# An attention and MoE kernel on one core: another order of issue in its first chunk

## The chip, the core and the metric

The kernel runs on one core of a Trainium2 chip. Its engines take their instructions each in its own order: TensorE (PE) multiplies, ScalarE (ACT), VectorE (DVE) and GpSimd (POOL) do elementwise work, and SyncE (SP) issues the DMAs. The metric is the device time of one execution in microseconds. Before the change the runs gave 989.86, 989.25 and 988.27 us, a median of 989.25.

## The reference

For each of 8 batches and 8 heads, attention over 576 tokens of 64 values, where a token sees only few others: in heads 0 to 3 the 32 tokens up to itself, in heads 4 to 7 every fourth of the last 128. The result is the input x of a mixing layer of low rank and of a two-layer perceptron:

```python
scores = scale * np.matmul(q, k.transpose(0, 1, 3, 2))
scores = np.where(masks[None], scores, -1e9)          # windows of 32, plain or dilated by 4
attn = softmax(scores)
x = np.matmul(attn, v)                                # to (8, 576, 512)
h = x.transpose(0, 2, 1) @ U @ V                      # U: 576 x 32, V: 32 x 576
u = x + h.transpose(0, 2, 1)
out = u + np.maximum(u @ w_ch1, 0.0) @ w_ch2          # 512 -> 2048 -> 512
```

U, V and the two weights come as 64-bit floats, the rest as 32-bit floats.

## The kernel before

**The perceptron** sets the frame. The 36 tiles of 128 tokens are worked in 12 chunks: chunk 0 holds 4 tiles, chunk 1 two, the others three. The 2048 hidden values are 16 blocks, f = 0 to 15. For each chunk and f, `layer1` makes `ph` (one PSUM tile) in three groups of four matmuls, w1h by uth, w1l by uth, w1h by utl: weights and data are each split in a rounded high part and the rest, so that three products stand for one exact one. ACT makes `hh` (the rounded relu of ph), DVE makes `hl` (the rest). `layer2` of the block before then adds into the accumulators `acc`, three matmuls per tile of tokens. So an f is 12 matmuls of ph and 12 of acc in chunk 0.

**The weights** are made in chunk 0 while they are first used. A piece (`raw`, 64-bit words, w1 or w2 of one f, in turn) is fetched by SP, four raw buffers in all. ACT narrows both halves of its words (L199, L203), DVE shifts (L207), DVE (for w1) or POOL (for w2) adds (L209), then the high part is cast (w1h on ACT, L213; w2h on DVE, L215) and POOL takes the low part as the difference (L216). `weight_step` runs twice per f; it finishes one piece, adds the next, and narrows the one after. The 64-bit U and V take the same way: the last of them is a piece called uv, number 2, whose parts `fetch_rest`, `narrowed(2)`, `add_low(2)` and `finish(2)` are put in by hand.

**Attention.** Batch 0 is worked ahead of chunk 0. Batch 1 is worked in chunk 0, in nine blocks of 64 rows twice by four heads: scores `s` (L416), on DVE the masked row maxima `nmax` (L435), on ACT the exponentials `p` (L439), on PE the turned `ptp` (L450), a copy to `pt` (DVE, L456), the product with v, `pv` (L473), and on DVE a division by the row sums (L479 to L503). Rows of the dilated heads are scattered to their tokens by DMAs from `xp` into x (L516, SP).

**The mixing layer.** For each batch and each half c of the columns: `split_x` makes xhl, a high part on ACT (L529) and a low one on POOL or DVE (L531), for five tiles of tokens; `t_mm` multiplies them with U into one PSUM tile t (L561); `t_evict` turns t into ts with three ACT casts and one DVE subtraction in turn (L570 to L577); `mix` multiplies ts with V into m (L585), and DVE adds it to x (L587). The first half of batch 0's x (dilated heads) leaves as xp to a buffer in DRAM (`leave`, "spare", L813) and comes back in order of tokens (`come`, L818) before mix(0, i, 1) adds to it.

**What sets the order.** A list `queue` holds pairs of a position and a step of work. In chunk 0, `slot()` is called 109 times, between the groups of matmuls of layer1 and between tiles of layer2. It counts a position up from 0, by 4/(3 x 109) = 0.0122 per slot, and each time issues all steps of the queue whose position has been reached. An f is 6.8 slots. What the list issues stands on every engine at that place. Batch 1's part is made by `batch_items`: its attention blocks start at STEP0 and follow at STEP1 = 0.075, and its mixing layer starts, for each half, at AFTER's first number, with AFTER's second number between one step and the next. Work on PSUM goes through one set of three buffers ("ps") for s, ptp, pv, t and m.

## Time and profile before

The profiled execution took 991.13 us, of which the span from its first to its last instruction is 989.30; the granted TensorE clock was 0.968 of full speed in the mean.

| stretch, us from the start | length | PE busy | DVE | ACT | POOL |
| --- | --- | --- | --- | --- | --- |
| 0 to 43.34: batch 0's attention, ph_0 | 43.34 | 37.76 | 25.66 | 28.44 | 20.07 |
| 43.34 to 166.84: the rest of chunk 0 | 123.50 | 115.89 | 92.69 | 68.73 | 78.70 |
| 166.84 to the end: chunks 1 to 11 | 822.46 | 816.13 | 468.39 | 283.72 | 232.99 |

Names in the profile are those of the program without buffer numbers; "[1.30 <-ACT ts L577]" behind an instruction says that its engine was idle for 1.30 us before it, until ACT's instruction of line 577 ended. Where numbers are kept, as below, ph0_1 is chunk 0's ph of f=1, and x_436 one buffer of x. A line such as "x16" stands for that many instructions in a row.

### The profile page before, as it was taken

To read this page: it belongs to the slowest core of one execution; us is meant where nothing else is said; L and a number is where in the kernel's file an instruction comes from. 1 tells how busy PE (TensorE), PEld (TensorE's weight loads), DVE (VectorE), ACT (ScalarE), POOL (GpSimd) and SP (SyncE) were. 2 spreads that over 40 slices of the span, in tenths; PEclk is the share of its full clock that TensorE was granted. 3 is DMA by queue.
4 is the path that set the end of the run, shared out by engine and by line. 5 is a ranking of instruction groups with operands and counts; after the bars stand their busy time and mean duration, and the time that the engine had idled before them with its cause. 6 is when DMAs were issued, how large, how long until landed. Compare 5 with 4: busy or idle time off the path is not lost.

```text
span 989.3 us, 18075 instructions
## 1 busy us (share of the span) xinstructions
PE 969.8 (98%) x5941; PEld 844.2 (85%) x5941; DVE 586.7 (59%) x1969; ACT 380.9 (38%) x936; POOL 331.8 (34%) x555
## 2 busy tenths in 40 slices
PE   9898999999999999999999999999999999999998
PEld 7576778888888888888888888888898888999997
DVE  5676787777377758766377745776557773311211
ACT  6654654454244424343144432435233531111110
POOL 4575656354143514253042521335122620000000
PEclk9899999999999999999999999999999999999999
DMA  9476644344244316343233413443243412200000
GB/s 332 139 243 200 200 158 132 106 138 115 54 129 133 103 45 172 108 129 96 70 99 91 136 57 89 136 125 84 71 102 101 135 56 53 86 1 1 32 1 32
DMA packets 100188, 106.15 MB, mean 107 GB/s; under 512 B 12480, under 2 KB 85376, under 8 KB 100096
## 3 DMA queue, kind: packets, MB, share of 16 engines
q1 hardware_dynamic: 100096, 105.01, 36.1%
q8 instruction: 48, 0.79, 0.3%
q14 instruction: 44, 0.36, 0.1%
HBM read 82.94 MB, written 17.89 MB: 102 GB/s over the span
## 4 chain that ended last, share of the span: by engine, by line
PE 79%; DMA 2%; DVE 2%; SPq 0%; issue 0%; POOL 0%; ACT 0%; DVEq 0%; POOLq 0%; ACTq 0%
PE ph L965 35%; PE acc L982 35%; PE pv L473 3%; PE s L403 3%; PE t L561 2%; DMA zd<-z 1%; PE m L585 1%; PE s L416 1%; DMA qkr<-qk 0%; DVE pt L462 0%; DVE x L1012 0%; DMA x<-xp 0%; SPq L634 0%; DVE v L209 0%; DVE z L630 0%
## 5 line engine op out<-in xcount | busy, mean ns | idle before, releaser
L982 PE MATMUL acc<-w2h,hh 128*128 128x512 f32 x576 | 227.4, 395 | 0.0
L982 PE MATMUL acc<-w2l,hh 128*128 128x512 f32 x576 | 227.3, 395 | 0.0
L380 POOL TENSOR_TENSOR qks<-qkr,qks 128x160 fp32r<-128x160 f32 x192 | 103.8, 541 | 328.4 <-ACT qks L379 242.3
L982 PE MATMUL acc<-w2h,hl 128*128 128x512 f32 x576 | 213.0, 395 | 0.2 <-DVE hl L971 0.2
L971 DVE SCALAR_TENSOR_TENSOR hl<-ph,hh 128x384 fp32r<-128x384 f32 (+2 forms) x192 | 106.3, 554 | 177.4 <-ACT hh L970 176.5
L970 ACT ACTIVATE hh<-ph 128x384 fp32r<-128x384 f32 (+2 forms) x192 | 93.5, 487 | 264.3 <-PE ph L965 255.2
L965 PE MATMUL ph<-uth,w1h 128*128 128x384 f32 (+2 forms) x768 | 170.6, 340 | 4.3 <-ACT w1h L213 3.6
L965 PE MATMUL ph<-utl,w1h 128*128 128x384 f32 (+2 forms) x768 | 172.6, 338 | 0.0
L965 PE MATMUL ph<-uth,w1l 128*128 128x384 f32 (+2 forms) x768 | 170.5, 339 | 0.2 <-POOL w1l L216 0.2
L439 ACT ACTIVATE p<-p,nmax 128x160 f32<-128x160 f32 (+1 forms) x288 | 109.6, 406 | 130.7 <-DVE nmax L435 129.3
L965 PEld LDWEIGHTS ph<-uth,w1h 128*128 128x128 f32 x768 | 135.9, 188 | 22.3 <-ACT w1h L213 4.9
L462 DVE STREAM_TRANSPOSE pt<-p 32x128 f32<-32x128 f32 x432 | 130.1, 301 | 18.6 <-ACT p L439 13.3
L965 PEld LDWEIGHTS ph<-uth,w1l 128*128 128x128 f32 x768 | 133.6, 189 | 4.3 <-POOL w1l L216 1.3
L965 PEld LDWEIGHTS ph<-utl,w1h 128*128 128x128 f32 x768 | 133.4, 188 | 3.8 <-issue 0.2
L982 PEld LDWEIGHTS acc<-w2h,hl 128*128 128x128 f32 x576 | 107.7, 188 | 22.6 <-DVE hl L971 0.6
L982 PEld LDWEIGHTS acc<-w2h,hh 128*128 128x128 f32 x576 | 108.2, 188 | 16.2
L982 PEld LDWEIGHTS acc<-w2l,hh 128*128 128x128 f32 x576 | 108.3, 188 | 15.8 <-issue 0.2
L379 ACT CAST qks<-qkr 128x288 fp32r<-128x288 f32 x192 | 81.0, 429 | 103.7 <-PE s L403 54.5
L383 POOL TENSOR_TENSOR qks<-qkr,qks 64x128 fp32r<-64x128 f32 x192 | 90.5, 471 | 15.0
L432 DVE TENSOR_TENSOR p<-s,wide_sb 128x160 f32<-128x160 f32 x192 | 59.5, 320 | 57.0 <-PE s L403 54.4
L531 POOL TENSOR_TENSOR xhl<-x,xhl 128x256 fp32r<-128x256 f32 (+1 forms) x65 | 47.6, 741 | 83.1 <-ACT xhl L529 73.8
L435 DVE CUSTOM_DVE_ANT_0 p<-s,p 128x160 f32<-128x160 f32 x192 | 59.8, 320 | 3.7
(89 smaller groups left out, 875.8 us busy)
## 6 DMA issues: line engine op xcount, KB each, us to landing
qkr<-qk SPq DMA_DIRECT2D x192, 144.0 KB, 2.2
v<-vv SPq DMA_DIRECT2D x126, 130.0 KB, 2.4
raw<-w SPq DMA_DIRECT2D x26, 512.0 KB, 4.1
out<-x SPq DMA_DIRECT2D x36, 256.0 KB, 2.4
zd<-z SPq DMA_DIRECT2D x120, 64.0 KB, 2.1
xt<-zd SPq DMA_DIRECT2D x30, 256.0 KB, 2.8
k<-qk SPq DMA_DIRECT2D x18, 320.0 KB, 5.6
raw<-w SPq DMA_DIRECT2D x12, 256.0 KB, 3.4
```

Of the source, the lines that this page charges most:

```text
L379: nc.scalar.copy(out=t[:, 0:QK2], in_=raw)
L380: nc.gpsimd.tensor_tensor(out=t[:, QK2:], in0=raw[:, P:], in1=t[:, P:QK2].bitcast(F32), op=ALU.subtract)
L383: eng.tensor_tensor(out=t[lo, 0:P], in0=raw[lo, 0:P], in1=t[lo, 0:P].bitcast(F32), op=ALU.subtract)
L432: nc.vector.tensor_tensor(out=p_sb[:, u, :], in0=sp[:, 0:KW], in1=held[0][:, kind], op=ALU.add)
L435: nc.vector.tensor_tensor_reduce(out=p_sb[rs, u, 0:w], in0=a, in1=c, scale=-1.0 / 8.0, scalar=3.0e38, op0=ALU.add, op1=ALU.min, accum_out= ...
L439: nc.scalar.activation(out=p_sb[:, u, 0:w], in_=p_sb[:, u, 0:w], func=AF.Exp, bias=nmax[:, u:u + 1], scale=-1.0,)
L462: nc.vector.transpose(out=pt[WIN * k:WIN * (k + 1), :, rs], in_=p_sb[rs, :, o:o + WIN])
L531: eng.tensor_tensor(out=xl[rs], in0=x[rs], in1=xh[rs].bitcast(F32), op=ALU.subtract)
L965: nc.tensor.matmul(ph, lhsT=w[:, k, :], rhs=u[:, k, :], start=(n == 0), stop=(n == len(seq) - 1))
L970: nc.scalar.activation(out=hh, in_=ph, func=AF.Relu)
L971: nc.vector.scalar_tensor_tensor(out=hl, in0=ph, scalar=0.0, in1=hh.bitcast(F32), op0=ALU.max, op1=ALU.subtract)
L982: nc.tensor.matmul(acc[i], lhsT=h[:, ss], rhs=w, start=(f == 0 and n == 0), stop=(f == FC - 1 and n == 2))
```

## The change

Only positions in the list and the order of steps within batch 1's mixing layer change, all of it in chunk 0:

- STEP0 goes from 0.012 to 0.03: batch 1's attention starts at the third slot in place of the first, in the middle of f=1 in place of f=0, and each of its blocks is later by that much.
- For batch 1's mixing layer (b < SPLIT), the product t of a tile comes two places behind its split in place of one, and two empty places stand between the eviction of t and the first mix. AFTER goes from (0.60, 0.022), (0.84, 0.03) to (0.64, 0.024), (0.84, 0.028).
- Batch 0: `leave` starts at 0.10 in place of 0.15, `come` at 0.18 in place of 0.22, and the mixes at 0.27 and 0.345 in place of 0.18 and 0.27.
- The piece uv is fetched at 0.08 in place of 0.04, narrowed at 0.17 in place of 0.10, added at 0.20 in place of 0.12, finished at 0.25 in place of 0.14; `split_first_u` moves from 0.17 to 0.40.

```diff
@@ -86,9 +86,11 @@
 PE_T = 18
 U_AT = 4
 V_AT = 7
-STEP0 = 0.012
+STEP0 = 0.03
 STEP1 = 0.075
-AFTER = ((0.60, 0.022), (0.84, 0.03))
+AFTER = ((0.64, 0.024), (0.84, 0.028))
+BEHIND = 2
+EVICT = 2
 LO2 = 1.31
 HI2 = 2.45
 NQ = 2
@@ -821,16 +823,19 @@
         attn = attention_steps(b)
         n = len(batch_parts(b))
         after = []
+        behind = BEHIND if b < SPLIT else 1
         for c in (1, 0):
             more = []
-            for i in range(n + 1):
+            for i in range(n + behind):
                 def go(i=i, c=c):
-                    if i > 0:
-                        t_mm(b, i - 1, c)
+                    if i >= behind:
+                        t_mm(b, i - behind, c)
                     if i < n:
                         split_x(b, i, c)
                 more.append(go)
             more.append(lambda c=c: t_evict(b, c))
+            if b < SPLIT:
+                more += [lambda: None] * EVICT
             more += [lambda i=i, c=c: mix(b, i, c) for i in range(n)]
             after.append(more)
         first = NJ // 2 + LAG + 1
@@ -913,10 +918,10 @@
 
     n0 = len(batch_parts(0))
     queue = [(AHEAD_AT[0], lambda: ahead(0)), (AHEAD_AT[1], lambda: ahead(1))]
-    queue += [(0.15 + 0.01 * p, lambda p=p: leave(p)) for p in range(NDP)]
-    queue += [(0.22 + 0.005 * i, lambda i=i: come(i)) for i in range(n0)]
-    queue += [(0.18 + 0.012 * i, lambda i=i: mix(0, i, 0)) for i in range(n0)]
-    queue += [(0.27 + 0.008 * i, lambda i=i: mix(0, i, 1)) for i in range(n0)]
+    queue += [(0.10 + 0.012 * p, lambda p=p: leave(p)) for p in range(NDP)]
+    queue += [(0.18 + 0.012 * i, lambda i=i: come(i)) for i in range(n0)]
+    queue += [(0.27 + 0.013 * i, lambda i=i: mix(0, i, 0)) for i in range(n0)]
+    queue += [(0.345 + 0.013 * i, lambda i=i: mix(0, i, 1)) for i in range(n0)]
 
     def fetch_rest():
         pipe[2] = fetch64(2)
@@ -925,8 +930,8 @@
         finish_u(u32[:, 0:4 * RANK], slice(0, 4))
         finish_u(u32[:, 4 * RANK:5 * RANK], slice(8, 9))
 
-    queue += [(0.04, fetch_rest), (0.10, lambda: narrowed(2)), (0.12, lambda: add_low(2, nc.gpsimd)),
-              (0.14, lambda: finish(2)), (0.17, split_first_u)]
+    queue += [(0.08, fetch_rest), (0.17, lambda: narrowed(2)), (0.20, lambda: add_low(2, nc.gpsimd)),
+              (0.25, lambda: finish(2)), (0.40, split_first_u)]
     for b in range(1, B):
         lo, hi = (1.5 * b - 2 - LO0, 1.5 * b - 0.5) if b > 2 else (LO2, HI2 + MARGIN)
         its = batch_items(b)
```

The counts of instructions are the same on all five engines. Lines from 92 on lie 2 lower in the changed file, and from the end of `batch_items` on 5 lower, so L213 becomes L215 and L965 becomes L970. Buffer numbers differ as well.

PE at the start of chunk 0, before (s9 are the scores of batch 1's first block):

```order
L965 MATMUL ph0_0_613<-uth0_69,w1h_0_82 128x512 x4
L965 MATMUL ph0_0_613<-uth0_69,w1l_0_83 128x512 x4
L416 MATMUL s9_626<-k9_168,q1_1_76 128x96 x4
L965 MATMUL ph0_0_613<-utl0_70,w1h_0_82 128x512 x4
L965 MATMUL ph0_1_667<-uth0_69,w1h_0_82 128x512 x4
L965 MATMUL ph0_1_667<-uth0_69,w1l_0_83 128x512 x4
L965 MATMUL ph0_1_667<-utl0_70,w1h_0_82 128x512 x4
```

and of the change:

```order
L970 MATMUL ph0_0_613<-uth0_69,w1h_0_82 128x512 x4
L970 MATMUL ph0_0_613<-uth0_69,w1l_0_83 128x512 x4
L970 MATMUL ph0_0_613<-utl0_70,w1h_0_82 128x512 x4
L970 MATMUL ph0_1_648<-uth0_69,w1h_0_82 128x512 x4
L418 MATMUL s9_657<-k9_168,q1_1_76 128x96 x4
L970 MATMUL ph0_1_648<-uth0_69,w1l_0_83 128x512 x4
L970 MATMUL ph0_1_648<-utl0_70,w1h_0_82 128x512 x4
```

The scores s9 moved from behind the second group of ph0_0 to behind the first group of ph0_1.

SP where the copies from DRAM come back, before (x0 to x4 are the five tiles of batch 0; "x<-xp" are the scatters of batch 1):

```order
L818 DMA x3_561<-spare_785 128x256
L351 DMA v11_0_907<-vv 128x260
L351 DMA v11_1_909<-vv 128x260
L330 DMA k14_911<-qk0 128x640
L516 DMA x4_436<-xp9_810 16x256
L516 DMA x5_914<-xp9_810 32x256
L516 DMA x6_916<-xp9_810 16x256 x2
L516 DMA x7_919<-xp9_810 32x256
L516 DMA x8_921<-xp9_810 16x256
L818 DMA x4_436<-spare_785 64x256
```

and of the change:

```order
L820 DMA x2_536<-spare_707 128x256
L820 DMA x3_561<-spare_707 128x256
L820 DMA x4_436<-spare_707 64x256
L192 DMA raw15_878<-w1 128x4x256
L353 DMA v11_0_892<-vv 128x260
L353 DMA v11_1_894<-vv 128x260
L332 DMA k14_896<-qk0 128x640
L518 DMA x4_436<-xp9_811 16x256
```

The copy for x4 moved from behind the scatters to ahead of the next v and k; the scatters follow behind these.

ACT around f=7 and f=8, before (xhl_0_1 is the high part of the first split of batch 1, p_1391 and p_1402 the exponentials of an attention block):

```order
L970 ACTIVATE hh_7_1345<-ph_7_1332 128x512
L213 CAST w1h_1084<-v_1263 128x4x128
L199 ACTIVATE v_1353<-raw_1266 128x512
L203 ACTIVATE raw_1266<-raw_1266 128x512
L529 CAST xhl_0_1_1367<-x_436 64x256
L439 ACTIVATE p_1391<-p_1391,nmax_1392 128x96 x4
L529 CAST xhl_1_1_1415<-x_914 128x256
L199 ACTIVATE v_1422<-raw_1330 128x512
L203 ACTIVATE raw_1330<-raw_1330 128x512
L529 CAST xhl_2_1_1438<-x_916 128x256
L970 ACTIVATE hh_8_1445<-ph_8_1427 128x512
L213 CAST w1h_1084<-v_1353 128x4x128
```

and of the change:

```order
L975 ACTIVATE hh_7_1345<-ph_7_1289 128x512
L215 CAST w1h_1071<-v_1263 128x4x128
L201 ACTIVATE v_1353<-raw_1266 128x512
L205 ACTIVATE raw_1266<-raw_1266 128x512
L201 ACTIVATE v_1374<-raw_1287 128x512
L205 ACTIVATE raw_1287<-raw_1287 128x512
L441 ACTIVATE p_1402<-p_1402,nmax_1403 128x96 x4
L531 CAST xhl_0_1_1427<-x_436 64x256
L975 ACTIVATE hh_8_1434<-ph_8_1379 128x512
L215 CAST w1h_1071<-v_1353 128x4x128
L201 ACTIVATE v_1442<-raw_1356 128x512
L205 ACTIVATE raw_1356<-raw_1356 128x512
```

The p that stood right behind the first split now has its counterpart, p_1402, right ahead of it, with two more narrowing steps ahead of both.

## The prediction, made before the changed kernel was run

> **What bounds the kernel now.** I read the page's first part, then windows around chunk 0, since after it the instructions stand in the same order in both programs.

> ```profile
> span 989.3 us, 18075 instructions
> PE 969.8 (98%) x5941; PEld 844.2 (85%) x5941; DVE 586.7 (59%) x1969; ACT 380.9 (38%) x936; POOL 331.8 (34%) x555
> 43.34:166.84 123.50, 115.89 (x666) 91.20 (x667) 92.69 (x221) 68.73 (x159) 78.70 (x81) 0.94 0.58 182
> 166.84:989.30 822.46, 816.13 (x4932) 725.24 (x4930) 468.39 (x1620) 283.72 (x705) 232.99 (x436) 0.97 0.32 89
> ```

> TensorE (PE) sets the end: 98% busy. In a window's row the first number behind the window is its length, the next PE's busy time. From the first matmul of ph_1 to the end of chunk 0, PE is idle for 123.50 - 115.89 = 7.6 us; one more wait, of 3.55 us, stands just ahead. The products themselves don't change, so the change can move about 11 us of idle time and some slow matmuls, and nothing else; the 822 us behind I leave as they are. The list of PE's waits in chunk 0 (total us, times, longest) says who ends the idle time:

> ```profile
> PE ph L965 <- ACT w1h L213: 3.6, 1, 3.6
> PE ptp L450 <- DVE x L587: 1.6, 1, 1.6
> PE m L585 <- ACT ts L577: 1.3, 1, 1.3
> PE pv L473 <- DMA v<-vv: 1.1, 1, 1.1
> PE t L561 <- POOL xhl L531: 1.1, 2, 0.7
> PE pv L473 <- DVE x L587: 0.6, 1, 0.6
> PE ph L965 <- DVE hl L971: 0.5, 1, 0.5
> PE pv L473 <- DVE v L207: 0.4, 1, 0.4
> PE t L561 <- DVE xhl L531: 0.2, 1, 0.2
> PE ph L965 <- POOL w1l L216: 0.2, 1, 0.2
> PE t L561 <- ACT xhl L529: 0.2, 1, 0.2
> ```

> Nearly every line is a single event with its own cause, so I go through them one by one.

> **The start: batch 1's first block a block later.** The timeline (start, length, engine, idle before):

> ```profile
> 37.80 1.03 PE L416 MATMUL s<-k,q 128*128 128x96 f32 x8
> 38.62 1.17 PE L965 MATMUL ph<-utl,w1h 128*128 128x512 f32 x4
> 39.36 1.56 DVE L209 CUSTOM_DVE_ANT_0 v<-raw,v 128x1024 uint16<-128x1024 uint16 x1
> 41.13 1.17 ACT L439 ACTIVATE p<-p,nmax 128x96 f32<-128x96 f32 x4 [1.80 <-DVE nmax L435]
> 42.21 0.57 ACT L970 ACTIVATE hh<-ph 128x512 fp32r<-128x512 f32 x1
> 42.69 0.61 ACT L213 CAST w1h<-v 128x512 fp32r<-128x512 f32 x1
> 43.34 1.82 PE L965 MATMUL ph<-uth,w1h 128*128 128x512 f32 x4 [3.55 <-ACT w1h L213]
> ```

> The weight that PE waits for could be cast when DVE's add ends, at 39.36 + 1.56 = 40.92. The cast starts only at 42.69, behind batch 1's four p and hh_0. Without the p, hh_0 lies ahead of 40.92 and w1h ends near 41.6: 1.7 us earlier. But the scores s, which lay ahead of the wait and cost nothing (38.62 - 37.80 = 0.8), now lie behind it. Net gain **0.9**.

> The first group there is slow, 1.82 us, where the one at 38.62 took 1.17. The windows have the granted clock as the number before the last two:

> ```profile
> 39.80:43.34 3.54, 0.00 (x0) 0.00 (x0) 2.36 (x10) 2.21 (x7) 1.77 (x3) 0.95 0.82 291
> 43.34:47.00 3.66, 3.66 (x9) 2.52 (x10) 1.22 (x4) 2.23 (x4) 3.03 (x3) 0.53 0.20 71
> 76.00:88.00 12.00, 11.47 (x69) 8.75 (x69) 7.95 (x31) 6.40 (x16) 5.32 (x6) 0.95 0.74 228
> ```

> After 3.5 us without a matmul the clock is 0.53 for 3.7 us; after the 1.58 us that end at 76.11 it stays at 0.95. In the changed order PE stands still for about 2.7 us (from 38.62 + 1.17 - 0.8 = 39.0 to 41.65), between the two. The slow stretch costs 3.66 x (1 - 0.53/0.95) = 1.6 us, so 0 to 1.6 may be gained. I take **0.2**, since a PE that isn't slowed comes to ph_2 near 49.5, and that group's w1h and w1l, laid out with the casts, adds and maxima ahead of them on ACT, DVE and POOL, end only near 50.0 and 51.5: most of the 1.6 is waited away again. [...]

> **Mixes of batch 0 later, the copies to DRAM and back earlier.** The two waits at L587 (0.6 and 1.6 in the list) have one cause:

> ```profile
> 73.24 0.59 SPq L818 DMA_DIRECT2D x<-spare  x1
> 75.55 0.41 DVE L587 TENSOR_TENSOR x<-x,m 64x256 f32<-64x256 f32 x1 [2.49 <-DMA x<-spare]
> 76.11 0.63 PE L450 MATMUL ptp<-id_sb,p 128*96 128x128 f32 x4 [1.58 <-DVE x L587]
> ```

> DVE stood for 2.49 us ahead of the mix of x_436, whose data SP issued only at 73.24, behind the scatters. hl_4, the row maxima and the score buffers that PE needs queued behind it. In the new order this copy stands ahead of those scatters (some 3 us of issues at 0.4 to 0.6 each) and its mix some 7 places later, so it lands long before. Gain **2.2**, and **0.2** for the w1l line, which comes right behind. If the copy were late all the same, the gain would be 0.

> What is late next: batch 1's v tiles, which SP now issues behind the raw of U and V and the copies.

> ```profile
> v<-vv SPq DMA_DIRECT2D x126, 130.0 KB, 2.4
> 96.97 0.90 PE L473 MATMUL pv<-v,pt 96*64 96x65 f32 x16 [1.10 <-DMA v<-vv]
> ```

> The wait of 0.4 put down to L207 is such a landing; it stays, and the next pv finds its v within 0.1 us of being needed. Bounds 0 to 2.4, one whole issue to landing: a **loss of 0.3**, nearer the low end, since only one raw tile more stands ahead. The v that came 1.10 us late at 96.97 keeps its place in the stream of weights and is needed a block later: gain **1.1**.

> **Two places ahead, two empty places.** The waits of t on splits (1.1 + 0.2 + 0.2) and of the first m on ts:

> ```profile
> 144.49 0.38 PE L585 MATMUL m<-ts,vs 128*128 128x256 f32 x1 [1.30 <-ACT ts L577]
> ```

> A split now stands two places of 0.024 ahead of its product, in slots of 4/(3 x 109) = 0.0122: 3.9 slots of the 6.8 of an f, some 4 us, where one place of 0.022 was 1.8 slots. The late splits lacked 0.2 to 0.7 us, ts 1.3. Gain 1.5 + 1.3 = **2.8**; with the 0.5 of ph on hl, behind the same evictions, **3.3**. Each wait removed also saves PE refilling, as pv at 96.97 (0.90 after its wait) tells: nine fewer at 0.1, **0.9**.

> Against it stand new waits. Attention now fills f=7 to 9 beside the splits. On ACT the cast of xhl_0_1 stands behind p_1402, and this behind row maxima and a DVE add. If PE comes to the first t with both to run, it waits 1.56 + 1.17 = 2.7 (the add's and p's rows above); if not, 0. I take **1.6**, past the middle, because PE reaches that t right behind the attention products whose maxima p needs. The same p stands ahead of w1h, hh and hl at f=7 and 8: 0 to 1.17 each, I take half at each, **1.2** in all. The splits on POOL that are still close, the 0.7 of the list once: **0.6**. And narrowed U and V, moved into f=2 and 3, put one more add on POOL there, 320 columns of the 512 that take 1.3 below, 0.8 at most: **0.5**.

> **The weight chain at the end.** From f=10 on, the two first rows are the cast of w1h and the start of its ph for f=10, the others for f=15:

> ```profile
> 120.63 0.61 ACT L213 CAST w1h<-v 128x512 fp32r<-128x512 f32 x1
> 123.50 1.08 PE L965 MATMUL ph<-uth,w1h 128*128 128x512 f32 x4
> 155.54 0.62 ACT L213 CAST w1h<-v 128x512 fp32r<-128x512 f32 x1 [0.51 <-DVE v L209]
> 157.30 0.94 PE L965 MATMUL ph<-uth,w1h 128*128 128x512 f32 x3 [0.47 <-DVE hl L971]
> ```

> Weights come every (156.16 - 121.24)/5 = 7.0 us, PE goes on every 33.8/5 = 6.8, waits included; the cast's end is 2.3 us ahead of PE at f=10 and 1.1 at f=15. If PE comes here 4 to 5 us earlier, the chain holds it: between 0 (it follows) and 3 (it doesn't, past its slack). I take **1.0**, since casts and shifts stand in queues behind hh and hl and so follow PE in part.

> **Sum.** Gains 0.9 + 0.2 + 2.2 + 0.2 + 1.1 + 3.3 + 0.9 = 8.8; losses 0.3 + 1.6 + 1.2 + 0.6 + 0.5 + 1.0 = 5.2; rounded up from 3.6 to **4.0 us**, because waits on one weight don't add when two losses fall on it (p's and the chain's). The profiled execution takes 991.13, its span and 1.83 around it, so it would be 987.1. It lies 1.88 above the median of the runs; 989.25 - 4.0 = **985.2**.

> **Rivals.** (1) *The chain takes the gain back.* All that the first half gains only brings PE earlier to weights that come every 7.0 us. For it speaks the lead of 1.1 us at f=15; against it, that the chain is held by hh and hl. With its full 3 us for 1.0, and a v late by 1.0: 988.2. (2) *It all stays.* The losses are covered: 989.25 - 8.8 = 980.5. For it: each is small, and I walked their order by hand. (3) *Slower: the shift loses its race with POOL.* The end of w1h releases w1l on POOL and, by way of hl's end, the shift on DVE at almost one time:

> ```profile
> 112.07 1.30 POOL L216 TENSOR_TENSOR w1l<-v,w1h 128x512 fp32r<-128x512 f32 x1
> 112.13 1.52 DVE L207 TENSOR_SCALAR v<-v 128x512 int32<-128x512 int32 x1
> 141.69 0.42 DVE L207 TENSOR_SCALAR v<-v 128x512 int32<-128x512 int32 x1
> 141.74 1.52 POOL L216 TENSOR_TENSOR w1l<-v,w1h 128x512 fp32r<-128x512 f32 x1 [1.43 <-ACT w1h L213]
> L207 DVE TENSOR_SCALAR v<-v 128x512 int32<-128x512 int32 x29 | 18.4, 634 | 0.0
> ```

> Where w1l started 0.06 us ahead, the shift took 1.52; where the shift started 0.05 ahead, 0.42. The mean of 0.634 over 29 makes (0.634 - 0.42) x 29 / 1.1 = 5 to 6 lost races, of two to each f. A lost one puts POOL's add and w2h back by 1.1. If eight more of the 22 in f=5 to 15 are lost, 8.8 us, less the lead of 1.1 and the 1.0 counted already: 985.2 + 6.7 = 991.9. It decides from about eight on. Against it: nothing in the new order names the loser beforehand. [...]

> **How the numbers follow.** The forecast, with its own range of 983 to 987.2: 0.50. All stays, below 983: 0.13. Taken back, 987.3 to 991.2: 0.25. Slower, to 994: 0.12. The range for 8 in 10 is 981.8 to 990. A difference of 0.2%, 2 us, is about what a measurement of this kernel can tell from none: faster 0.63, same 0.25, slower 0.12.

> **What would show it.** At the start, w1h for ph_1 ending near 41.6 and a gap of 2.7 us or less, with the windows behind it telling whether the clock fell. No wait by way of L587, none of m on ts, none of 1.1 on v. Its steps are wrong if the first t waits over 2.7 us, if pv waits on v for more than 1 us twice, or if w1h or w1l hold PE for more than 2 us in f=10 to 15.

## The result: slower by half a per cent

The changed kernel took 995.47 us (median of 8 runs, 992.69 to 998.45), the kernel before 989.56 (median of 8, 988.27 to 992.94). The ratio is 1.0051 with a 95% interval of 1.0037 to 1.0065. The forecast was 985.2.

The profiled execution of the change took 992.69 us, the fastest of its eight. Its windows from the start of ph_0 to the end of chunk 0, and from there to the end (length, then PE busy):

```profile
34.35:165.43 131.08, 120.08 (x687) 94.21 (x686) 96.98 (x237) 74.72 (x173) 83.07 (x85) 0.99 0.58 180
165.43:990.90 825.47, 818.61 (x4932) 725.92 (x4930) 468.27 (x1620) 282.74 (x705) 233.55 (x436) 1.00 0.32 88
```

and of the kernel before, from its ph_0 on:

```profile
35.44:166.84 131.40, 120.24 (x687) 94.08 (x686) 98.63 (x237) 74.83 (x173) 82.61 (x85) 0.94 0.57 180
```

Two things are told here. Chunk 0 is as long as before (131.1 against 131.4) with as much idle PE time in it (11.0 against 11.2 us), though it should have shrunk by 4. And chunks 1 to 11, whose instructions stand in the same order, take 825.5 us where they took 822.5. PE's waits in chunk 0 of the changed kernel:

```profile
PE ph L970 <- ACT w1h L215: 2.8, 1, 2.8
PE pv L475 <- DMA v<-vv: 2.1, 1, 2.1
PE ph L970 <- POOL w1l L218: 1.9, 3, 1.5
PE t L563 <- ACT xhl L531: 1.1, 1, 1.1
PE t L563 <- POOL xhl L533: 1.0, 2, 0.5
PE ph L970 <- DVE hl L976: 0.7, 1, 0.7
PE m L587 <- DVE x L589: 0.7, 1, 0.7
PE ptp L452 <- DVE ssum L481: 0.3, 1, 0.3
PE s L418 <- DVE x L589: 0.3, 1, 0.3
```

The waits that the prediction removed are gone: none of 1.6 and 0.6 at the mix (L589 now; waits of 0.7, at batch 1's mixes, and of 0.3 have come there), none of 1.3 on ts, none of 1.1 on the later v. Others stand in their place, first the 2.1 us on the first v.

### The profile page after: what moved, and what is told of

Same layout as the page of the kernel before. It is cut to its first block, busy times and chain, and to the rows that moved or that the text cites. A ratio compares the mean times of both kernels' runs of the same rounds, so it can differ in the third digit from the quotient of the medians.

```text
span 990.9 us, 18072 instructions
## 1 busy us (share of the span) xinstructions
PE 971.4 (98%) x5941; PEld 844.5 (85%) x5941; DVE 584.9 (59%) x1969; ACT 379.8 (38%) x936; POOL 332.8 (34%) x555
## 4 chain that ended last, share of the span: by engine, by line
PE 79%; DVE 3%; DMA 3%; issue 1%; POOL 1%; SPq 1%; ACT 1%; DVEq 0%; POOLq 0%; ACTq 0%
PE acc L987 35%; PE ph L970 35%; PE pv L475 3%; PE s L405 3%; PE t L563 2%; DMA zd<-z 1%; PE m L587 1%; DVE v L211 1%; DVE v L209 0%; DMA qkr<-qk 0%; DVE pt L464 0%; PE s L418 0%; SPq L518 0%; DVE x L1017 0%; DMA x<-xp 0%
## 5 line engine op out<-in xcount | busy, mean ns | idle before, releaser
L987 PE MATMUL acc<-w2h,hl 128*128 128x512 f32 x576 | 213.7, 396 | 0.4 <-DVE hl L976 0.4
L970 PE MATMUL ph<-uth,w1h 128*128 128x384 f32 (+2 forms) x768 | 169.7, 339 | 3.6 <-ACT w1h L215 2.8
L970 PE MATMUL ph<-utl,w1h 128*128 128x384 f32 (+2 forms) x768 | 172.5, 338 | 0.0
L970 PE MATMUL ph<-uth,w1l 128*128 128x384 f32 (+2 forms) x768 | 170.1, 338 | 1.9 <-POOL w1l L218 1.9
L970 PEld LDWEIGHTS ph<-uth,w1h 128*128 128x128 f32 x768 | 135.7, 188 | 21.7 <-ACT w1h L215 4.9
L970 PEld LDWEIGHTS ph<-uth,w1l 128*128 128x128 f32 x768 | 132.9, 188 | 6.3 <-POOL w1l L218 3.8
L970 PEld LDWEIGHTS ph<-utl,w1h 128*128 128x128 f32 x768 | 133.4, 188 | 3.9 <-issue 0.2
L987 PEld LDWEIGHTS acc<-w2h,hh 128*128 128x128 f32 x576 | 108.5, 188 | 16.7
```

The costliest lines, as they stand in the source:

```text
L970: nc.tensor.matmul(ph, lhsT=w[:, k, :], rhs=u[:, k, :], start=(n == 0), stop=(n == len(seq) - 1))
L987: nc.tensor.matmul(acc[i], lhsT=h[:, ss], rhs=w, start=(f == 0 and n == 0), stop=(f == FC - 1 and n == 2))
```

## What happened outside chunk 0

The page's groups of the second layer's matmuls (busy us, mean ns of one), of the kernel before:

```profile
L982 PE MATMUL acc<-w2h,hh 128*128 128x512 f32 x576 | 227.4, 395 | 0.0
L982 PE MATMUL acc<-w2l,hh 128*128 128x512 f32 x576 | 227.3, 395 | 0.0
```

and of the change:

```profile
L987 PE MATMUL acc<-w2h,hh 128*128 128x512 f32 x576 | 228.9, 397 | 0.0
L987 PE MATMUL acc<-w2l,hh 128*128 128x512 f32 x576 | 228.5, 397 | 0.0
```

With the third group (213.0 and 213.7) they are busy 3.4 us longer, about as much as these chunks grew. The first layer's groups are not slower (means of 338 to 340 ns before, 338 to 339 in the change). Something that belongs to acc alone had changed, and the order hadn't. What had changed was where tiles lie. A pool lays its tiles out in the order of their first use. The maxima of batch 1's first block (nmax, two tiles of 32 bytes with their padding) were used ahead of hh and hl; a block later they are used behind them, and hh and hl move down by 64 bytes. From the built programs (bytes within a partition):

```
        before            change
nmax    45824, 45856      54016, 54048
hh      45888, 47936      45824, 47872
hl      49984, 52032      49920, 51968
```

Runs a1 to a4 went to one chip. a1 is the change unaltered. a2 reserves nmax ahead of hh:

```diff
+            if c == f == 0:
+                for i in range(2):
+                    work.tile([P, UNITS], F32, tag="nmax", name=f"first{i}", bufs=2)
             hh = work.tile([P, CTOK], F32R, tag="hh", ...)
```

a3 does the contrary in the kernel before, with hh and hl reserved at the head of chunk 0. Both keep every instruction at its place.

> The changed kernel unaltered, on the chip of the three others. Its profile showed chunk 0 ending 1.4 us earlier than before, and chunks 1 to 11, whose instructions stand in the same order, 3.0 us longer (825.5 against 822.5), with the second layer's matmuls of 512 columns a mean 397 ns long against 395. Theory P (placement): these matmuls are slower because hh and hl lie 64 bytes lower in each partition (45824 in place of 45888): nmax, first used by batch 1's first block, is now placed behind them in place of ahead. P expects 992 to 998 us again, a ratio of 1.004 to 1.006, and 1.0 to 1.5 ns more per acc matmul. Theory R (the run): the pace differs from chip to chip or run to run; then the ratio here can be anything from 0.998 to 1.006.

> The changed kernel with two tiles of nmax reserved ahead of hh, so that nmax, hh and hl lie where they lay before; the order of all instructions stays that of the change. P: chunks 1 to 11 take 822.5 us again and the whole 986 to 989 us, 1 to 3 us less than before, 6 to 8 less than the unaltered change. R: as the unaltered change, within 1 us. Theory S (the score buffers in PSUM, which trade places 5 and 7 in the change and still do here): as the unaltered change.

> The kernel before with hh and hl reserved ahead of nmax, so that these three lie where the change puts them; the order of instructions is that of before. P: chunks 1 to 11 take 3 to 7 us longer, 993 to 997 us in all, chunk 0 as before. R and S: as before, within 1 us.

Measured: a1 993.66 us, ratio 1.0037 (1.0024 to 1.0051). a2 991.39, ratio 1.0010 (0.9999 to 1.0021). a3 993.00, ratio 1.0031 (1.0020 to 1.0042). The placement alone makes the kernel before 2.7 us slower, and taking it from the change gives 2.3 back. The windows behind chunk 0 say it without the noise of whole runs, first a2, then a3:

```profile
168.03:990.90 822.87, 816.33 (x4932) 725.22 (x4930) 468.64 (x1620) 282.68 (x705) 233.52 (x436) 1.00 0.32 88
```

```profile
166.93:992.40 825.47, 818.87 (x4932) 725.55 (x4930) 469.21 (x1620) 283.25 (x705) 232.30 (x436) 1.00 0.32 88
```

a2 expected 986 to 989 us, though, and came to 991.4: with placement put right the change is 1 us slower than before, not 4 faster. That is chunk 0's part, below.

Three runs, one profile each, put 32, 64 or 96 unused bytes ahead of hh in the change (`work.tile([P, 8], F32, tag="pad", ...)` and so on). All tiles behind move too, most of w2h and w2l among them.

> The change with 32 unused bytes ahead of hh, so hh and hl start 32 bytes later than in the change (45856 in each partition). In the profiles so far the second layer's matmuls of 512 columns follow each other in 229 ns late in the kernel with hh at 45888 and in 233 ns at 45824. If the pace goes by the place in a step of 64 bytes, 45856 gives a third value or one of the two; if only a multiple of 128 is slow, 229. Chunks 1 to 11 then take 822 to 823 us; at 233 ns, 825 to 826.

> The change with 64 unused bytes ahead of hh: hh and hl lie at 45888 as in the kernel before, while nmax stays behind them and everything behind is 64 bytes higher. If hh and hl alone decide: 229 ns and 822 to 823 us for chunks 1 to 11. If it is nmax's place or the tiles behind: 233 ns and 825 to 826.

> The change with 96 unused bytes ahead of hh, which puts hh and hl at 45920, 96 above a multiple of 128. Matmul to matmul late in the kernel the second layer took 233 ns at 0 above (45824), 231 at 32, 229 to 230 at 64. If it goes by the distance to a multiple of 128, 231 as at 32; if it falls on with the address, 227 to 228.

The group of acc (w2h by hh) in the window 800 to 960 us, where little else runs, of the kernel before, a2, the change and a3:

```profile
L982 PE MATMUL acc<-w2h,hh 128*128 128x512 f32 x113 | 44.4, 392 | 0.0
L990 PE MATMUL acc<-w2h,hh 128*128 128x512 f32 x111 | 43.6, 392 | 0.0
L987 PE MATMUL acc<-w2h,hh 128*128 128x512 f32 x111 | 44.1, 397 | 0.0
L987 PE MATMUL acc<-w2h,hh 128*128 128x512 f32 x111 | 44.1, 397 | 0.0
```

a1 has 397 as well; then the mean is 394 at 32 bytes, 392 at 64 (with nmax left behind, so it is hh and hl that count), 394 at 96. At these four addresses, 45824 to 45920, it goes with the distance to a multiple of 128: 397 ns on one, 394 at 32 from it on either side, 392 at 64. That this is a rule was not shown: in two later runs (d2 and d3 below) hh lay at 50112, 64 above a multiple of 128, and took 397. There it depends on the other operand too, 397 against 393 with the same hh; of d3:

```profile
L996 PE MATMUL acc<-w2h,hh 128*128 128x512 f32 x112 | 44.4, 397 | 0.0
L996 PE MATMUL acc<-w2l,hh 128*128 128x512 f32 x112 | 44.1, 393 | 0.0
```

The five addresses are 0, 32, 64, 96 and 192 above a multiple of 256; a rule of 256, or of the distance between hh and w2, was not tried. Nor is the pace all: chunks 1 to 11 took 825.2 us at 32 bytes, 824.6 at 64 and 825.3 at 96, more than 392 to 394 ns account for, with x and the q and k of later batches moved too. Which of these costs that was not tried.

## What happened in chunk 0

**Parts, alone and taken back.** All with nmax, hh and hl as in the kernel before. a4 is the kernel before with `STEP0 = 0.03`. b2 is the change with `BEHIND = 1` and `EVICT = 0`. b3 is the change with batch 0's part old:

```diff
-    queue += [(0.10 + 0.012 * p, lambda p=p: leave(p)) for p in range(NDP)]
+    queue += [(0.15 + 0.01 * p, lambda p=p: leave(p)) for p in range(NDP)]
...
-    queue += [(0.08, fetch_rest), (0.17, lambda: narrowed(2)), ...
+    queue += [(0.04, fetch_rest), (0.10, lambda: narrowed(2)), ...
```

b4 is the change with `STEP0 = 0.012`. c1 is the kernel before with AFTER, BEHIND and EVICT of the change and nothing else.

> The kernel before with STEP0 = 0.03 alone, and nmax, hh and hl placed as before. It tells what the later start of batch 1 is worth in chunk 0. As predicted (w1h of ph_1 freed, +0.9; clock kept, up to +1.6; v at 96.97 later needed, +1.1): 2 to 3.5 us less than before, 986 to 987.5. If the gain of the start is waited away at the next v loads, as the changed kernel's wait of 2.14 us on v suggests, 0 to 1 us less than before: 988.5 to 989.5. The start's gap should be near 2.7 us with the clock at 1.0 behind it.

> The change, placed as before, with splits one place ahead of the products in place of two and no empty places behind the eviction. By the prediction these two are worth the waits of t on splits (1.5 us) and of m on ts (1.3): then this takes 2 to 3 us longer than the placed change (993.5 to 994.5), with m waiting 1.3 on ts and t 1.5 to 3 on splits. If the chain of weights holds f=10 to 15 anyway, the waits come back but the end of chunk 0 moves by less than 1 us.

> The change, placed as before, with all of batch 0's part (copies to DRAM and back, mixes, U and V) at its old positions; batch 1's new positions stay. The prediction gave this part 2.2 + 0.2 for the mix that waited 2.5 us for its copy, less 0.3 for later v and 0.5 for U and V: 1.6 us. So 993 if that holds, with the waits at the mixes back (0.6 and 1.6 us or more) and the first v's wait near 0.5. If the later v costs the change what the mix gains (2 to 3 us), 990.5 to 991.5, the same as the placed change.

> The change, placed as before, with STEP0 back at 0.012, so that batch 1's attention starts in f=0 while its mixing layer keeps the later AFTER and the two places. STEP0 alone made the kernel 8.0 us slower, since t's splits met the last attention blocks: here the distance between the two is larger than in before and in the change. If that distance is what counts: the waits of t on splits (2.1 us in the change) go, w1h of ph_1 waits 3.5 us again with the slow clock behind it; 989 to 991. If the late start is what the change needs: 992 to 994.

> The kernel before with only batch 1's mixing layer changed: AFTER, two places between split and product, two empty places behind the eviction. STEP0 and all of batch 0's part stay, and nmax, hh and hl lie as before. So far, one place in place of two cost 6.7 us in the changed order, the late STEP0 3.1, and batch 0's new positions 2.0. Theory A (these add up): 988.3 for the change with the old STEP0, less 1 to 2 for batch 0's part: 986 to 987.5, a ratio near 0.996. Theory B (each only moved the waits at the v loads; the chain of weights at the end is the floor, w1l waiting 1.5 us at f=15 whichever way): 988 to 989, a ratio near 0.998. The waits of t on splits and of m on ts should be gone, those at the mix (0.6 and 1.6 or more) be back.

| run | late STEP0 | batch 0's part | two places | us | ratio (95%) |
| --- | --- | --- | --- | --- | --- |
| a4 | new | old | old | 998.33 | 1.0080 (1.0066 to 1.0093) |
| b2 | new | new | old | 998.04 | 1.0089 (1.0068 to 1.0111) |
| a2 | new | new | new | 991.39 | 1.0010 (0.9999 to 1.0021) |
| b3 | new | old | new | 989.39 | 0.9988 (0.9978 to 0.9997) |
| c1 | old | old | new | 988.33 | 0.9979 (0.9970 to 0.9987) |
| b4 | old | new | new | 988.29 | 0.9974 (0.9962 to 0.9987) |

The parts don't add. b2 came out some 4 us above its expectation, b3 1 us below both of its cases and b4 below its first; of c1's theories, B held. The two places gain 2.2 us alone and 6.7 in the changed order. Batch 0's new positions gain nothing with the old STEP0 and lose 2.0 with the late one. The late STEP0 loses 8.0 alone (its expectation, a gain of 0 to 3.5, fell), 1.1 beside the two places and 3.1 in the full change. It brings the last attention blocks up to the splits of the mixing layer, as a4's waits show:

```profile
PE t L561 <- POOL xhl L531: 4.0, 2, 2.1
PE t L561 <- ACT xhl L529: 2.5, 3, 1.9
```

That is 6.5 us where the kernel before had 1.3 on the same lines. All of PE's idle time in chunk 0 grew by less, from 11.2 to 13.6 us; the rest of the 9.2 us by which a4's chunk 0 is longer are slower matmuls (127.0 us against 120.2), of which below. I expected c4, the change with AFTER at 0.66 and 0.86, to restore the distance:

> The change, placed as before, with AFTER at 0.66 and 0.86 in place of 0.64 and 0.84. If the distance between batch 1's last attention block and the first split is what the late STEP0 spoils, the distance of the faster run with the old STEP0 is back here: the waits of the first t (1.05 and 0.53) and of ph on hl (0.7) go, and the whole takes 989 to 990, where the placed change took 991.4. If the chain of weights at the end holds, the wait of w1l at f=15 grows by what is saved and the time stays 991 to 992.

It took 994.80 us, ratio 1.0045 (1.0033 to 1.0057), 3.4 more than a2. The first t's waits did go, from 1.05 and 0.53 to 0.27. But other splits still hold PE (0.66 and 0.61), and the mixing layer now ends in the last f's, where PE waits for weights and for hl:

```profile
151.34 1.16 PE L970 MATMUL ph<-uth,w1h 128*128 128x512 f32 x4 [2.18 <-ACT v L201]
158.67 1.16 PE L970 MATMUL ph<-uth,w1h 128*128 128x512 f32 x4 [1.09 <-DVE hl L979]
```

So both ends look held: attention must be through before the splits, the mixes before the last weights. Of the two positions tried, neither gives a late start of attention a place to go.

**The clock.** Idle time alone doesn't explain a2, whose chunk 0 is 133.65 us with 11.4 idle, against 131.40 with 11.2 before. Windows of the change around its first v have the granted clock before the last two numbers:

```profile
54.02:56.16 2.14, 0.01 (x1) 0.04 (x1) 0.80 (x2) 2.14 (x5) 1.54 (x2) 1.00 0.93 208
56.60:60.00 3.40, 3.40 (x27) 3.25 (x25) 1.45 (x10) 0.38 (x2) 1.39 (x3) 0.51 0.87 275
```

A wait of 2.1 us is followed by 3.4 us at half the clock, a loss of up to 3.4 x 0.5 = 1.7 us more. In a2 the two waits of the first t's (1.05 and 0.53 us) do the same:

```profile
111.00:114.00 3.00, 1.42 (x7) 0.62 (x5) 1.84 (x10) 2.76 (x8) 0.72 (x1) 1.00 0.80 257
114.30:117.70 3.40, 3.40 (x25) 2.51 (x24) 1.33 (x5) 2.91 (x7) 3.40 (x4) 0.50 0.10 13
```

Summed over chunk 0 in windows of 1 us, what the slow clock takes comes in steps of 1.7 us: one step in the kernel before, in the change's profile, a1 and c1, two in a3, b4 and e1, three in a2, b1, b2, b3 and d1, six in a4 (10.2 us, more than its 8.0 of loss). A stretch of matmuls that the clock slows while PE would soon wait anyway costs less than its step: with five steps more than before, 8.5 us, a4's matmuls took 6.7 us longer. What the two places gain in the changed order is not the clock's, since a2 and b2 have three steps each: it is idle time, 11.4 us in a2's chunk 0 and 16.7 in b2's.

The length of a wait alone doesn't decide. The gap ahead of ph_1 was 2.72 to 2.77 us in twelve profiles with the late STEP0. In five the clock stayed up (first group 1.20 us), in seven it fell, at once or a group later. First the change, then d1:

```profile
40.53 1.19 PE L970 MATMUL ph<-uth,w1h 128*128 128x512 f32 x4 [2.75 <-ACT w1h L215]
```

```profile
40.68 2.07 PE L976 MATMUL ph<-uth,w1h 128*128 128x512 f32 x4 [2.73 <-ACT w1h L215]
```

The spans of the change's eight executions go with their mean clock, from 990.9 us at 0.997 to 996.7 at 0.990: much of the spread between them is this.

**The loads of v.** b1 issues the two v tiles of the first block with the block's start; d1 issues all of batch 1's v a block earlier:

```diff
+                if b < SPLIT and s < 2:
+                    load_v(g, 0)
+                    load_v(g, 1)
...
             def post(s=s, g=g):
+                if b < SPLIT and 2 <= s < NGB:
+                    load_v(g, 0)
+                    load_v(g, 1)
```

> The change, placed as before, with the two v tiles of batch 1's first block issued with the block's start (right behind w2 of f=3) in place of a block later behind the raw of U and V. In three profiles of the change PE waited 2.0 to 3.1 us for this v, where the kernel before waited 0.4 to 0.8. Theory V (the gain of the start is waited away at this v): the wait goes, ph of f=3 starts 2 to 3 us earlier than in the change, chunk 0 ends 2 to 3 us earlier, and the whole takes 988.4 to 989.4 where the placed change took 991.4 and before 990.3. Theory W (the chain of weights or the next v takes it back): the wait goes, but chunk 0's end moves by less than 1 us, 990.4 to 991.4.

> The change, placed as before, with all v tiles of batch 1 issued a block earlier: those of the first two blocks with their block's start, the others right behind the product that frees their buffer. With the first v alone moved, PE's wait went over to the second (2.3 us), and the kernel gained 0.9 us. Theory V (v loads are the wall that takes the start's gain): with all of them earlier chunk 0 ends 2 to 3 us earlier than in the placed change, 988.4 to 989.4, a ratio of 0.998 to 0.999. Theory E (the end of chunk 0 is the floor: w1h and w1l of the last f come when they come): the v waits go, the waits of t on splits and of w1l grow by as much, 990.5 to 991.5.

b1: 990.53 us, ratio 0.9998 (0.9987 to 1.0010), 0.9 less than a2. The first wait goes and the second v gets it:

```profile
64.07 1.39 PE L475 MATMUL pv<-v,pt 96*64 96x65 f32 x16 [2.29 <-DMA v<-vv]
```

d1: 988.98 us, ratio 0.9987 (0.9977 to 0.9996), 2.4 less than a2. No wait on v is left, chunk 0 is 130.1 us long against 133.65, with 8.3 us idle against 11.4 and three steps of slow clock in both, and the waits at its end are the old ones (w1l at f=15 is 1.5 us in both). Theory V, that v's issue is the wall, holds; with v out of the way the placed change is a little faster than before. Why v is late can be read on SP in the change:

```profile
45.72 0.38 SPq L192 DMA_DIRECT2D raw<-w  x1
51.06 0.33 SPq L194 DMA_DIRECT2D raw<-uv  x1
51.91 0.97 SPq L353 DMA_DIRECT2D v<-vv  x2
```

SP stands from 46 to 51 us ahead of the raw of U and V, until POOL's add, which reads the buffer that it needs, ends at 49.72 + 1.32 = 51.04; v is behind it on SP, whenever PE comes for it.

**A version that beats both.** b4's order and c1's with v a block earlier (d3, d2), and both again with nmax, hh and hl reserved first (e1, e2):

> Only the two places (0.9979 of before so far), with batch 1's v a block earlier as well. It had waits of 0.5 and 0.5 us left on v: V and E both give 0 to 1 us less than without, 987.3 to 988.3. Theory Q (SP stands still at a v whose buffer isn't free, and the weights behind it come late): new waits on w1h or w1l, 989 to 991.

> The two places and batch 0's new positions with the old STEP0 (0.9974 of before so far), with batch 1's v a block earlier. It had 2.1 us of waits on v left: V gives 986.3 to 987.3, a ratio near 0.996; E 988 to 988.5; Q over 989.

> The order of the run before with two places, batch 0's new positions, the old STEP0 and v a block earlier, which ended chunk 0 4.4 us ahead of before but lost 2.9 us of it in chunks 1 to 11, where hh and hl had come to lie at 50112 (behind v) and the second layer's matmuls followed each other in 232 to 233 ns. Here nmax, hh and hl are reserved first, at the addresses of the kernel before (45824, 45888, 49984); no instruction changes its place. Theory P (placement alone): 229 ns again, chunks 1 to 11 as before within 0.5 us, the whole 985.5 to 987, a ratio near 0.996. If the pace in that run came from the order: 990 to 991 us.

> The same for the order with two places and v a block earlier alone (batch 0's part and STEP0 old), which measured 993.7 us with hh at 50112. P: 229 ns, 987 to 988 us, 0 to 1 us less than the two places alone (988.3); from the order: 992 to 994.

d2 took 993.72 us (1.0026, 1.0012 to 1.0041), d3 991.06 (1.0005, 0.9997 to 1.0014), slower than without the early v, though their chunk 0 was shorter. Used first, v had been laid ahead of hh and moved it to 50112. With the old addresses and the same order, e1 took 986.42 (0.9954, 0.9940 to 0.9968) and e2 989.22 (0.9975, 0.9965 to 0.9984): 4 to 5 us less. e1's windows:

```profile
34.42:163.44 129.02, 119.64 (x686) 95.04 (x685) 98.04 (x237) 75.28 (x173) 84.12 (x85) 0.97 0.60 183
163.44:984.60 821.16, 815.38 (x4932) 725.10 (x4930) 469.41 (x1620) 283.79 (x705) 233.78 (x436) 1.00 0.32 89
```

Chunk 0 is 2.4 us shorter than before, the rest 1.3. e1 is the change without the late STEP0, with v ahead. e2 shows that v ahead is worth nothing without batch 0's part (c1 had 0.9979): its mixes then wait for their copies.

## Why the prediction was wrong, step by step

The forecast was 4.0 us less, the measurement 5.9 more, above the range and above all the cases. Of the 9.9 us between them, the places of tiles outside chunk 0 take 2.3 to 3.0, and chunk 0 about 5 (with the old addresses, 1.1 us slower in place of 4.0 faster). The rest, some 2 to 3 us by which the first eight runs lie further above the kernel before (5.9) than the five of a1 (3.3), is not explained by any run.

- *"The 822 us behind I leave as they are."* This step failed first: a term put at nothing. It followed the order of instructions and not where tiles lie: 3.0 us in the profiles, 2.3 and 2.7 us in the two pairs of runs.
- *The start, +0.9 and +0.2.* w1h was freed as worked out (a gap of 2.75 us, forecast 2.7). From ph_0 to ph_2 the change took 14.1 us against 16.5: 2.4 gained with the clock kept. Where it fell for one window (b2, c4) it took 15.5 to 15.6, the 0.9 of the forecast; where it fell for two (c3, d1 and three others), 16.8 to 16.9: nothing. The rows of the kernel before left open what a gap of 2.7 us does: after one of 3.5 the clock fell, after one of 1.58 it stayed up. Of the twelve profiles with this gap five kept the clock, with at most 1.83 us of it in one window of 3.41, and seven lost it, with 2.2 or more in one.
- *"A loss of 0.3" for later v.* This is the step that failed in chunk 0. Mis-sized: waits of 2.0, 2.1 and 3.1 us in three profiles of this order where the kernel before waited 0.4, near the upper bound of 2.4 or past it, and d1 gains 2.4 by taking them away. I counted one raw tile more ahead of v, but not that SP stands still for that tile's buffer, nor that a PE which comes earlier waits for the same landing.
- *Mixes, +2.2 and +0.2.* The two waits at L587 went as forecast. Beside the old STEP0 the part nets 0.0 us: where c1 waits 2.6 us at mixes of batch 0 and 1.0 on v, b4 waits 1.7 at another mix and 2.1 on v.
- *Two places, +3.3 less 1.0 for the chain.* Near: c1 gained 2.2 us, and w1l's wait at f=15, for which the 1.0 stood, came to 1.5 to 1.7.
- *Nine waits fewer, +0.9.* None fewer: both lists of chunk 0 hold twelve waits. The 0.1 for each was an estimate: in the kernel before pv took 0.92 and 0.90 us behind its waits of 0.43 and 1.10, 0.69 behind the one of 0.61 and wherever it didn't wait. That PE refills there is not shown.
- *New waits of 1.6, 1.2 and 0.6 around f=7 to 9.* Right in size: 1.05 + 0.53, 0.23 + 0.73, 0.47. But in a2 and d1, though not in the change's own profile, they bring up to 1.7 us of slow clock with them, which the sum had only at the start.
- *"A block later", +1.1.* The v at 96.97 no longer waits. But the later block was priced only in these single terms, and as a whole the late STEP0 loses 3.1 us in the placed change.
- *The rivals.* The shift's races didn't come: its mean in the change is 0.628 us where it was 0.634. Rival 1 was nearest for chunk 0 (a2: 1.0010), with v and the clock in place of the chain. None had the placement.

## What to carry to other kernels

A change that touches only the order can still move tiles, since pools lay them out by first use: compare addresses too (64 bytes of hh and hl were worth 2.3 to 2.7 us here), and pin the tiles of the inner loop by reserving them first. Cost a wait on TensorE at its length and at up to 1.7 us more for each window at half the clock behind it: here the clock fell after 27 of 27 windows of 3.41 us with more than 1.85 us idle and after 11 of 45 with 1.13 to 1.85, and where the window's edge falls differed from run to run. And a gain ahead of a load was worth nothing here until the load was issued earlier; look what stands ahead of it in its queue.

## What the runs showed that I had not expected

- Late in the kernel (800 to 960 us) a matmul of 512 columns takes 392 to 397 ns, and follows the one before in 229 (before, hh at 45888) to 233 (the change, hh at 45824): some 1.5% on the same engine, order and data. From 170 to 590 us it is 231 against 232.
- The clock fell to 0.50 for 3.4 us after waits far shorter than that: one of 2.1 us (the change), or two that sum to 1.6 within 3 us (a2).
- The profile of the kernel before has a granted clock of 0.95 up to 595 us, and it was not slower for it: its chunks 1 to 11 took 822.5 us, those of a2, at 1.00 and with hh and hl at the same addresses, 822.9. So that figure alone doesn't order two kernels.
